# A spectral filter mixed with a 32-head expert lookup: smaller first loads, one transform table, one more row buffer, another order at the end

## The chip, the cores and the metric

One core of one Trainium2 chip runs the kernel. The metric is the device time of one execution in microseconds, the median over several runs. Inputs and output lie in the chip's memory; nothing is computed on the host besides the rearrangement of the inputs and the tables of cosines and sines.

## What is computed

`x` is 2048 x 576. One branch is a two-dimensional spectral filter: forward transform, a product with complex weights, transform back. The other branch is a lookup of experts: for each of 32 heads a query is scored against two lists of 64 keys, the best key of each list gives one row of 4096 (`u` and `v`, 576 numbers each), and gelu(x . u row) times the v row is added up over the heads. A gate per position mixes the two.

```python
g = sigmoid((x * gate_w).sum(-1, keepdims=True))
a = irfft2(rfft2(x) * (w_r + 1j * w_i))
q = einsum("nd,dhc->nhc", x, w_q)                 # 32 heads, 2 halves of 128
i1, i2 = argmax(q1 @ k1.T), argmax(q2 @ k2.T)     # 64 keys each
e = i1 * 64 + i2
b = sum_h gelu(x . u[e]) * v[e]
return g * a + (1 - g) * b
```

## The kernel before

**Tiles.** The 2048 positions are 16 tiles of 128. The first ten (`E_T`) are early tiles, the last six (`L_SEQ`) late tiles, worked on in three pairs (10,11), (12,13), (14,15). The heads are eight chunks of four.

**Score stage.** `load_x` brings 512 positions of one 128-row slice of x transposed; ScalarE writes a rounded high part and VectorE the rest (L356-362). `load_wq` and `build_m` multiply one slice of `w_q` with the keys (L352, L381-397): eight matmuls, a ScalarE copy `mh` (L396), a VectorE remainder `ml` (L397). There are five slices of the 576 inputs; the fifth has only 64 rows, and before the change those are stored twice, so that the fifth slice is loaded as 128 rows. `scores` (L402-455) multiplies, takes the maximum, and turns it into row numbers `ei`.

**Groups.** `group(t, c, ...)` (L480-540) handles one tile and one chunk of four heads. GpSimd gathers four times 128 rows of u and v (590 KB each, L487) into a ring of row buffers: `NG` = 12 plus `NG2` = 1 of the late pools, 13 late. VectorE forms four dot products (L496), ScalarE the gelu (L500), VectorE the factor `a` (L501). Then either VectorE adds the four v rows to the accumulator of the tile (L514), or, where `is_d` holds (even late tiles), ScalarE builds four diagonal matrices (L524) and TensorE adds up 16 matmuls per group in a PSUM tile `sums[t]`. For such a late tile ScalarE copies the PSUM tile to SBUF after the last chunk (L538).

**Spectral stage.** `fold` (L645) brings 16 tiles into the large buffer `BT`; ten `unit`s (L784) run the transforms along the positions with `f2`, `f4`, `f5`, `f6` and `unit_back`, and write `BT` again; `turns` (L677) loads two small tables per unit. `invert(t)` (L808-831) transforms one tile back along d: twelve matmul instructions, a ScalarE copy `pq` (L819), eight more against `krb`, two ScalarE copies scaled with the gate into `ga` (L830, L831). `mix(t)` (L833-836) is one VectorE instruction (L835) and the store. The tables along d, `t_fi`, are twelve planes: six for the way there (`fi[0]`), six with the scale of the way back (`fi[1]`).

**Order.** All work is entered in a planner (`Plan`, L105-233): each job has an engine, a cost, a due time `at` and its dependences. A simulation of the engines takes, on each engine, the ready job with the smallest due time for which buffers of its rings are free, and the order that comes out is written into the program; on the chip each engine and the queues of SP and POOL keep it. Due times of spectral work are spaced by `FPACE`, those of late groups by `TGS`. PSUM is a ring of four tiles of two banks (`p2`), shared by everything. In the time of the late work `xl` is a ring of six buffers, which hold the six late tiles of x and, when one is free, the `ga` of a late tile. Inversions come in the order early tiles, late tiles (L848).

Of the kernel before, what the change touches and what calls it, by code (L numbers as in the profile page):

```python
# [32 lines left out]
def _tables():  # L33
# [10 lines left out]
    def rows(fn, ds):  # L44
        return fn(2 * np.pi * np.outer(ds, k) / D)

    z = np.zeros((P, DF))
    ct = z.copy()
# [4 lines left out]
    fwd = np.stack([  # L53
        rows(np.cos, np.arange(0, 128)), rows(np.cos, np.arange(128, 256)), ct,
        -rows(np.sin, np.arange(0, 128)), -rows(np.sin, np.arange(128, 256)), -st,
    ])
    ck = np.full(DF, 2.0)
    ck[0] = ck[-1] = 1.0
    ck /= S * D

    def irows(fn, ks):
        return fn(2 * np.pi * np.outer(ks, k) / D) * ck[ks][:, None]

    ct = z.copy()
    ct[:33] = irows(np.cos, np.arange(256, 289))
    st = z.copy()
    st[64:96] = irows(np.sin, np.arange(256, 288))
    inv = np.stack([
        irows(np.cos, np.arange(0, 128)), irows(np.cos, np.arange(128, 256)), ct,
        irows(np.sin, np.arange(0, 128)), irows(np.sin, np.arange(128, 256)), st,  # L70
# [12 lines left out]
        "t_fi": c(np.concatenate([fwd, inv]).transpose(1, 0, 2)),  # L83
        "t_f4": c(f4),
        "t_f6": c(f6),
# [167 lines left out]
def tile_kernel(ctx, tc, xn, xT, wqT, kT, wri, uv, gw, t_kr, t_fi, t_f4, t_f6, t_io, out):  # L253
# [84 lines left out]
    gate = pp.tile([P, NT], F32, tag="gate", name="gate")  # L338
    gone = pp.tile([P, NT], F32, tag="gone", name="gone")
# [12 lines left out]
    def load_wq(c, i, at, after=()):  # L352
        w = wq_t[c, i] = buf("uv", ROW, view=lambda x: x.rearrange("p a d -> p (a d)")[:, : 8 * P].rearrange("p (g e) -> p g e", g=8))
        ld(load(P * 4096, 4096), at, lambda: nc.sync.dma_start(w.ap, wqT[c, i]), [w], after=after)

    def load_x(b, i, at, at2):  # L356
        st = buf("uv", ROW, view=lambda x: x[:, 0, :512])
        ld(load(P * 2048, 2048), at, lambda: nc.sync.dma_start(st.ap, xT[:, i, b * 512 : b * 512 + 512]), [st])
        hi = xts[i if i < 4 else 8][b]
        lo, r = (xts[4 + i][b], 0) if i < 4 else (hi, 64)  # L360
        ac(act(512), at2, lambda: actv(hi.ap, st.ap, AF.Copy), [hi], [st])
        dv(dve(512), at2, lambda: vt(lo.ap[r:], st.ap[r:], hi.ap[r:].bitcast(F32), ALU.subtract), [lo], [st, hi])
# [18 lines left out]
    def build_m(c, i, at, after=()):  # L381
        mh, ml = m_t[c, i] = [buf(n, [P, CW], F32R) for n in ("mh", "ml")]
        pm = psum()
        wq = wq_t[c, i]
        pv = lambda: pm.ap.rearrange("p a (g e) -> p (a g) e", e=128)

        def go():
            for g in range(8):
                half = g % 2
                mm(  # L390
                    pv()[:, g, :], wq.ap[:, g, :],
                    kTb.ap[:, half * 64 : half * 64 + 128], start=True, stop=True)
# [3 lines left out]
        ac(act(512), at, lambda: actv(v3(mh), pv()[:, :, :E], AF.Copy), [mh], [pm])  # L396
        dv(dve(512, True), at, lambda: vt(v3(ml), pv()[:, :, :E], v3(mh).bitcast(F32), ALU.subtract), [ml], [pm, mh])  # L397
# [4 lines left out]
    def scores(c, tp, at):  # L402
# [4 lines left out]
        def part(j, i):  # L407
            t = 2 * tp + j
            b = t // 4
            tsl = slice((t % 4) * P, (t % 4) * P + P)  # L410
            mh, ml = m_t[c, i]
            x = xts[i if i < 4 else 8][b]
            seq = [(x, mh), (x, ml)] + ([(xts[4 + i][b], mh)] if i < 4 else [])

            def go():
                for n, (xx, m) in enumerate(seq):
                    mm(ps.ap[:, j, :], xx.ap[:, tsl], m.ap, start=i == n == 0, stop=i == 4 and n == len(seq) - 1)

            use = {id(q): q for pair in seq for q in pair}
            return plan("PE", 0.23 * len(seq), at, go, [(ps, j)], list(use.values()))  # L420
# [59 lines left out]
    def group(t, c, at, ahead, gate_by=()):  # L480
        rows = []
        for k in range(HPC):
# [9 lines left out]
            rows.append(g)  # L492
        z, b, a = (buf(n, [P, HPC]) for n in ("z", "b", "a"))
        x = xs[t]
        for k in range(HPC):
# [3 lines left out]
        zk = [(z, k) for k in range(HPC)]  # L499
        ac(0.18, at - 9, lambda: actv(b.ap, z.ap, AF.Gelu_apprx_tanh), [b], zk, table="gelu")  # L500
        dv(0.08, at, lambda: stt(a.ap, b.ap, 1.0, sw[:, t, c * HPC : c * HPC + HPC], op0=ALU.mult, op1=ALU.mult),  # L501
           [a], [b, ("sw", t, c)])
        new = t not in accs
        if not is_d(t, c):
# [3 lines left out]
            for k in range(HPC):  # L508
# [8 lines left out]
        last = c == NCH - 1  # L517
        if part or t not in sums:
            sums[t] = psum()
        pd = sums[t]  # L520
# [11 lines left out]
        if part or last:  # L532
# [81 lines left out]
    for tag, pool, n in (  # L614
            ("t2", "ip", NT2), ("bt", "ip", 1), ("fi1", "ip", 1), ("krb", "ip", 1),
            ("uv2", "x2", NG2), ("xl", "x2", NT - NE), ("gr", "x2", 1),
            ("f5", "fp", 2), ("kr", "fp", 1), ("fi0", "fp", 1), ("t4", "fp", 2), ("t6", "fp", 2), ("w", "fp", 2)):
# [14 lines left out]
    fi = [buf("fi0", [P, 6, DF]), buf("fi1", [P, 6, DF])]  # L632
# [5 lines left out]
    ld(load(P * 6936, 4096), T0 + 8, lambda: nc.sync.dma_start(fi[0].ap, t_fi[:, 0:6, :]), [fi[0]])  # L638
    ld(0.5, T0 + 15, lambda: nc.sync.dma_start(gw2.ap, gw.partition_broadcast(P)), [gw2])
    ld(load(P * 6936, 4096), T0 + 90, lambda: nc.sync.dma_start(fi[1].ap, t_fi[:, 6:12, :]), [fi[1]])  # L640
# [4 lines left out]
    def fold(t, at):  # L645
        x = xs[t]
        f = buf("f5", [P, ND * P])
        ac(0.17, at, lambda: actv(f.ap[:, 0:385:384], x.ap[:, 0:1].to_broadcast([P, 2]), AF.Copy), [(f, 0)], [x])  # L648
# [15 lines left out]
    def f2(q, at):  # L664
        p = psum()

        def go():
            for r in range(2):
                for n, i in enumerate(((0, 1, 2), (3, 4, 2))[r]):
                    mm(p.ap[:, r, :DF], BT.ap[:, i, :, q], fi[0].ap[:, 3 * r + n, :], start=n == 0, stop=n == 2)  # L670

        plan("PE", 6 * pe(DF), at, go, [p], [fi[0], (BT, "q", q)] + [(BT, "in", t, i) for t in range(NT) for i in range(2)])
# [4 lines left out]
    def turns(k, at):  # L677
        t4 = buf("t4", [P, 3, P])
        t6 = buf("t6", [P, 5, P])
        ld(load(P * 1024, 1024), at - 8, lambda: nc.sync.dma_start(t4.ap[:, 0:2, :], t_f4[k]), [(t4, 0)])  # L680
        ld(load(P * 1024, 1024), at - 8, lambda: nc.sync.dma_start(t6.ap[:, 0:2, :], t_f6[k]), [(t6, 0)])
        ac(act(128), at - 2, lambda: actv(t4.ap[:, 2, :], t4.ap[:, 1, :], AF.Copy, scale=-1.0), [(t4, 1)], [(t4, 0)])
        ac(act(256), at - 2, lambda: actv(t6.ap[:, 2:5:2, :], t6.ap[:, 0:1, :].to_broadcast([P, 2, P]), AF.Copy), [(t6, 1)], [(t6, 0)])
        ac(act(128), at - 2, lambda: actv(t6.ap[:, 3, :], t6.ap[:, 1, :], AF.Copy, scale=-1.0), [(t6, 2)], [(t6, 0)])
        tabs[k] = t4, t6

    def f4(k2, X, at):
# [4 lines left out]
        t4, t6 = tabs[min(k2, 16 - k2)]  # L692
        a, b = (1, 2) if k2 <= 8 else (2, 1)
        p = psum()

        def go():
            T, x, o = t4.ap, X.ap, p.ap
            mm(o[:, 0, :DF], T[:, 0, :], x[:, 0, :], start=True, stop=False)
            mm(o[:, 0, :DF], T[:, a, :], x[:, 1, :], start=False, stop=True)
            mm(o[:, 1, :DF], T[:, 0, :], x[:, 1, :], start=True, stop=False)  # L700
            mm(o[:, 1, :DF], T[:, b, :], x[:, 0, :], start=False, stop=True)

        plan("PE", 4 * pe(DF), at, go, [p], [X, (t4, 0), (t4, 1)])
        return p, w, t6

    def f5(p, w, t6, at):
# [4 lines left out]
        dv(dve(DF), at, lambda: vt(a.ap[:, 0, :], a.ap[:, 0, :], b.ap[:, 1, :], ALU.subtract), [(a, 0)], [b])  # L711
        dv(dve(DF), at, lambda: vt(a.ap[:, 1, :], a.ap[:, 1, :], b.ap[:, 0, :], ALU.add), [(a, 1)], [b])  # L712
        return a, t6

    def f6(k2, zb, t6, at):
        pt = psum()
        u, v = (0, 3) if k2 <= 8 else (2, 1)

        def go():
            z, T = zb.ap, t6.ap  # L720
# [9 lines left out]
        plan("PE", 4 * pe(256) + 4 * pe(128), at, go, [pt], [(zb, 0), (zb, 1), (t6, 0), (t6, 1), (t6, 2)])  # L730
# [10 lines left out]
    def unit_front(k2, at):  # L741
# [8 lines left out]
        ac(act(DF), at, lambda: actv(sr.ap[:, 0, :], psn.ap[:, 1, :DF], AF.Copy, scale=-1.0), [(sr, 0), sr], [psn])  # L750
        ac(act(DF), at, lambda: actv(sr.ap[:, 1, :], psn.ap[:, 0, :DF], AF.Copy), [(sr, 1), sr], [psn])
# [4 lines left out]
    def unit_back(z, at):  # L756
# [19 lines left out]
        dv(dve(256, True), at, lambda: vt(tslot(qs, 0), tm()[:, 1], mainv(pb)[:, 1], ALU.subtract), [(BT, "q", qs, 0)], src + [s_])  # L776
        dv(dve(256, True), at, lambda: vt(tslot(qs, 1), mainv(pb)[:, 0], tm()[:, 0], ALU.subtract), [(BT, "q", qs, 1)], src + [s_])
# [3 lines left out]
        dv(dve(128, True), at, lambda: vt(BT.ap[0:33, 2, :, qs], ta.ap[64:97, 512:], pb.ap[64:97, 1, :P], ALU.subtract), [s_], src)  # L781
        dv(dve(128, True), at, lambda: vt(BT.ap[64:96, 2, :, qs], pb.ap[0:32, 1, :P], ta.ap[0:32, 512:], ALU.subtract), [s_], src)
# [147 lines left out]
```

## Time and profile before

| | |
|---|---|
| median of 3 runs | 1009.44 us (1008.35 to 1010.46) |
| the profiled execution's own time | 1001.24 us |
| its span | 999.5 us |
| mean granted TensorE clock | 0.965 |
| VectorE busy | 916.7 us, 92% of the span |
| TensorE busy | 904.4 us, 90% |
| GpSimd busy (issuing gathers) | 574.4 us, 57% |
| ScalarE busy | 514.6 us, 51% |
| moved by DMA | 348.39 MB, 302.02 MB of them gathered rows |

The profile comes from one execution. In tables of stretches, the columns are the stretch, its length, then for each engine its busy microseconds with the number of instructions begun (PE is TensorE, PEld its weight loads, DVE VectorE, ACT ScalarE, POOL GpSimd), the granted TensorE clock, the busy share of the DMA engines and the GB/s that they moved. In a timeline, a row is start, duration, engine, line and operation, and in brackets the idle time of the engine before it and what ended it. A list of waits gives who waited for whom, the total in us, how often, and the longest. A busy TensorE is not one at its peak, since ends of matmuls are modelled. Each fp32 matmul of the program stands as two instructions.

### The profile page before, as it was taken

The page shows a single profiled execution, that of the slowest core. Times are in us where ns is not written, and L with a number is a line of the kernel's source. Part 1 is how long each engine was busy: PE and PEld are TensorE (multiplying, and loading weights), DVE is VectorE, ACT ScalarE, POOL GpSimd, SP SyncE. Part 2 cuts the span into 40 slices and gives each one's busy share as a digit, 9 for nine tenths or more (in the row PEclk, how much of TensorE's full clock was granted, in tenths as well). Part 3 has the DMA queues.
Part 4 walks back from the last instruction along what each step waited for, and adds up shares of the span by engine and source line. Part 5 has one row for each costly group of instructions (what it writes and reads, how often), then busy time and mean ns, then how long its engine had stood idle before and what let it go on. Part 6 is the DMA issues. An engine that isn't in the chain of part 4 may idle for free. (4 is left out here: it accounts for less than half of the span.)

```text
span 999.5 us, 14406 instructions
## 1 busy us (share of the span) xinstructions
PE 904.4 (90%) x4208; PEld 735.8 (74%) x4208; DVE 916.7 (92%) x2255; ACT 514.6 (51%) x1877; POOL 574.4 (57%) x516
## 2 busy tenths in 40 slices
PE   8997999999999999999998990777999998899993
PEld 7885888878877888887877880665777776677762
DVE  3996999999999999999999999999999999977776
ACT  3874676676666576676666664522212222233331
POOL 0354656565656565755657566476655565676662
PEclk9997999999999999999999996889999999899998
DMA  9987999998989999998999799889999999999994
GB/s 336 336 286 301 349 361 367 358 352 305 392 309 361 371 344 332 395 345 328 386 360 330 291 394 378 340 312 389 394 357 351 357 353 321 349 390 414 398 359 192
DMA packets 93246, 348.39 MB, mean 349 GB/s; under 512 B 10480, under 2 KB 13296, under 8 KB 93168
## 3 DMA queue, kind: packets, MB, share of 16 engines
q0 software_dynamic: 73728, 302.02, 80.9%
q1 hardware_dynamic: 19440, 45.45, 12.3%
q8 instruction: 34, 0.56, 0.2%
q14 instruction: 44, 0.36, 0.1%
HBM read 342.71 MB, written 4.72 MB: 348 GB/s over the span
## 5 line engine op out<-in xcount | busy, mean ns | idle before, releaser
L487 POOL DMA_INDIRECT uv<-uv,ei x512 | 574.2, 1121 | 406.2 <-PE p L313 133.3
L313 PE MATMUL p<-mh,xt 128*128 128x512 f32 x1152 | 383.3, 402 | 9.1 <-ACT sg L435 7.3
L435 ACT ACTIVATE sg<-p,mx 128x64 bf16<-128x64 f32 x1024 | 225.8, 352 | 78.1 <-DVE mx L427 55.7
L514 DVE SCALAR_TENSOR_TENSOR xn<-uv,a,xn 128x576 f32<-128x576 f32 x322 | 262.0, 814 | 1.5
L313 PEld LDWEIGHTS p<-mh,xt 128*128 128x128 f32 x1152 | 218.4, 190 | 59.5 <-ACT sg L435 7.7
L313 PE MATMUL p<-ml,xt 128*128 128x512 f32 x640 | 253.2, 396 | 0.0
L496 DVE SCALAR_TENSOR_TENSOR uv<-uv,xn 128x576 f32<-128x576 f32 x320 | 236.3, 749 | 8.7 <-DMA uv<-uv,ei 6.8
L313 PE MATMUL p<-uv,dg 128*128 128x288 f32 x720 | 194.0, 425 | 29.3 <-ACT dg L524 22.5
L313 PEld LDWEIGHTS p<-uv,dg 128*128 128x128 f32 x720 | 140.8, 199 | 77.9 <-ACT dg L524 29.3
L496 DVE SCALAR_TENSOR_TENSOR uv<-uv,xl 128x576 f32<-128x576 f32 x192 | 141.5, 751 | 0.2
L313 PEld LDWEIGHTS p<-ml,xt 128*128 128x128 f32 x640 | 121.6, 190 | 26.6
L500 ACT ACTIVATE b<-z 128x4 f32<-128x4 f32 x128 | 26.4, 206 | 204.9 <-DVE uv L496 171.4
L313 PE MATMUL p<-fi,bt 128*128 128x289 f32 x384 | 97.7, 408 | 4.4 <-DVE t L710 3.0
L313 PEld LDWEIGHTS p<-fi,bt 128*128 128x128 f32 x384 | 83.5, 242 | 16.5 <-issue 3.7
L313 PEld LDWEIGHTS p<-kT,uv 128*128 128x128 f32 x640 | 77.8, 195 | 7.9 <-issue 4.8
L313 PE MATMUL p<-kT,uv 128*128 128x128 f32 x640 | 78.5, 279 | 5.0 <-DMA uv<-wqT 5.0
L427 DVE TENSOR_REDUCE mx<-p 128x16 f32<-128x1024 f32 x64 | 77.5, 1211 | 3.2 <-PE p L313 3.0
L313 PE MATMUL p<-t,t 128*128 128x289 f32 (+2 forms) x384 | 73.8, 362 | 5.9 <-issue 3.4
L446 ACT ACTIVATE sg<-sg 128x256 bf16<-128x256 bf16 x192 | 72.3, 427 | 1.2
L313 PEld LDWEIGHTS p<-t,t 128*128 128x128 f32 (+1 forms) x384 | 54.1, 165 | 23.9 <-issue 10.7
L524 ACT ACTIVATE dg<-ident,a 128x128 f32<-128x128 f32 x180 | 57.6, 393 | 17.7 <-DVE a L501 14.8
L313 PE MATMUL p<-kr,f 128*128 128x128 f32 x160 | 23.0, 301 | 31.5 <-ACT f L648 26.8
(86 smaller groups left out, 612.1 us busy)
## 6 DMA issues: line engine op xcount, KB each, us to landing
uv<-wqT SPq DMA_DIRECT2D x40, 512.0 KB
uv<-uv,ei POOLq DMA_INDIRECT x512
uv<-xT SPq DMA_DIRECT2D x20, 256.0 KB
w<-wri SPq DMA_DIRECT2D x16, 289.0 KB
out<-xn SPq DMA_DIRECT2D x16, 288.0 KB
xn<-xn SPq DMA_DIRECT2D x10, 288.0 KB
t<-t_f SPq DMA_DIRECT2D x18, 128.0 KB
fi<-t_fi SPq DMA_DIRECT2D x2, 867.0 KB
```

Source lines behind the costliest of these rows:

```text
L313: after("PE", nc.tensor.matmul(*args, **kw))
L427: dv(dve(1024, True), at, lambda: nc.vector.tensor_reduce(mv.ap[:, 2 * tp : 2 * tp + 2, :], ps.ap.rearrange("p a (g e) -> p a g e", e=E), ...
L435: on("ACT", actv(sg.ap[:, j, g, :], ps.ap[:, j, g * E : g * E + E], AF.Sign, bias=mv.ap[:, 2 * tp + j, g : g + 1], scale=-1.0))
L446: ac(act(256), at, lambda b=b: actv(s2()[:, :, b * Q : b * Q + Q], s2()[:, :, b * Q : b * Q + Q], AF.Copy, bias=b / 4), [sg], [])
L487: on("POOL", nc.gpsimd.indirect_dma_start(out=g.ap.rearrange("p a d -> p (a d)"), out_offset=None, in_=uv, in_offset=bass.IndirectOffsetOn ...
L496: dv(0.68, at, lambda k=k, g=rows[k]: stt(g.ap[:, 0, :], g.ap[:, 0, :], 1.0, x.ap, op0=ALU.mult, op1=ALU.mult, accum_out=z.ap[:, k : k + 1 ...
L500: ac(0.18, at - 9, lambda: actv(b.ap, z.ap, AF.Gelu_apprx_tanh), [b], zk, table="gelu")
L514: dv(0.73, at, lambda v=v, s=s: stt(y.ap, v(), s(), y.ap, op0=ALU.mult, op1=ALU.add), [y], [(rows[k], 1), a])
L524: ac(0.3, at - 9, lambda k=k, dg=dg: actv(dg.ap, ident, AF.Copy, scale=a.ap[:, k : k + 1]), [dg], [a, "ident"])
```

## The change

**First loads.** `w_q` and x transposed keep only the 64 rows of the fifth slice: that slice's loads are half as large. The key product of the fifth slice fills 64 partitions; ScalarE copies it twice, to both halves of `mh` (one ScalarE copy more per chunk), and `ml` and its score matmuls use 64 rows. Position blocks 2 and 3 come in one load each slice, and block 3 is split into its parts with block 2's due time (24) instead of its own (`when(3)`, 45.1).

**One table.** The six planes `fi` serve both ways; signs and factors of two move into additions, `fold`, `krb`'s use and a new scale `gsc` of the gate. One 867 KB load goes. The two tables of `turns` come in one load, `tw`.

**Buffers and pace.** The SBUF that becomes free holds one more late row buffer (`NG2` = 2, so 14). `FPACE` goes from 1.7 to 1.4.

**The end.** `INV` inverts late tiles first, then early ones. An even late tile is no longer copied out of PSUM: `mix` reads its `sums` there. The last group, tile 15 and chunk 7, is split in two pairs of heads (`LAST`) and comes after the mix of its tile: its rows are scaled with `gone`, 1 minus the gate, and added to the mixed tile. The store is a job of its own, `send`.

```diff
-        ac(act(512), at, lambda: actv(v3(mh), pv()[:, :, :E], AF.Copy), [mh], [pm])
+        for r in range(0, P, h):
+            ac(act(512), at, lambda r=r: actv(v3(mh)[r : r + h], pv()[:h, :, :E], AF.Copy), [(mh, r)], [pm])
...
     for i in range(ND):
-        load_x(2, i, 15, 24)
+        load_x(2, i, 15, 24, 2)
...
-    for i in range(ND):
-        load_x(3, i, 34, when(3))
...
-        if part or last:
+        if last and not part:
+            accs[t] = pd
+        elif part or last:
...
     def mix(t, at):
         ga, y = gas[t], accs[t]
+        if t in sums:
+            accs[t] = ga
+            half = lambda x: x.rearrange("p (r d) -> p r d", r=2)
+            dv(0.77, at, lambda: stt(half(ga.ap), y.ap[:, :, :288], gone[:, t : t + 1], half(ga.ap), op0=ALU.mult, op1=ALU.add),
+               [(ga, 0), (ga, 1), ga], [y, "gone"])
+            return
...
-    for n, t in enumerate(E_T + L_SEQ):
+    for n, t in enumerate(INV):
...
+        elif t % 2 == 0:
+            group(t, c, at, AHEAD, held)
+            mix(t, at + 9)
+            send(t, at + 9)
+        else:
+            mix(t, at - 4)
+            for ks in LAST:
+                group(t, c, at + 1.65 * ks[0], AHEAD, held, ks, True)
+            send(t, at + 9)
...
-NG2 = 1
+NG2 = 2
...
-FPACE = 1.7
+FPACE = 1.4
...
+INV = L_SEQ + E_T
+LAST = (0, 1), (2, 3)
```

More of the change, by code (lines that the diff above doesn't have):

```diff
@@ L52, in _tables @@
     st[64:96] = rows(np.sin, np.arange(256, 288))
[L53 to L70, printed above, removed]
+    fi = np.stack([
+        c0, rows(np.cos, np.arange(128, 256)), ct,
+        rows(np.sin, np.arange(0, 128)), rows(np.sin, np.arange(128, 256)), st,
     ])
@@ L478, in tile_kernel, with group @@
     sums = {}
-    def group(t, c, at, ahead, gate_by=()):
-        rows = []
-        for k in range(HPC):
+    def group(t, c, at, ahead, gate_by=(), ks=range(HPC), mixed=False):
+        rows = {}
+        for k in ks:
             g = buf(("uv", "uv2"), ROW)
@@ L516, in group @@
         part = t in E_T
[L517 to L520, printed above, removed]
+        last = not any(is_d(t, n) for n in range(c + 1, NCH))
+        if part:
+            pd = psum()
+        elif t in sums:
+            pd = sums[t]
+        else:
+            pd = sums[t] = psum()
         first = part or c == 0
```

172 lines of the change are left out of this document (94 added, 78 removed).

## Prediction

> **What bounds the kernel now.** I read the page's busy times first, then the run in stretches. Columns: stretch, length, busy microseconds of PE, PEld, DVE, ACT and POOL, the granted clock, DMA share, GB/s.
>
> ```profile
> 0.00:30.00 30.00, 25.04 (x142) 22.21 (x143) 11.82 (x18) 13.95 (x34) 0.20 (x4) 1.00 0.96 345
> 30.00:100.00 70.00, 62.48 (x299) 51.36 (x297) 60.20 (x156) 46.73 (x174) 33.52 (x32) 0.93 0.84 302
> 100.00:600.00 500.00, 490.21 (x2324) 401.90 (x2323) 489.13 (x1229) 333.80 (x1295) 305.56 (x269) 0.99 0.94 351
> 600.00:644.00 44.00, 15.70 (x101) 14.12 (x101) 43.73 (x114) 22.59 (x86) 25.75 (x21) 0.69 1.02 390
> 644.00:862.00 218.00, 191.08 (x870) 154.58 (x868) 210.62 (x507) 55.07 (x180) 130.73 (x120) 0.96 0.95 349
> 862.00:975.00 113.00, 109.93 (x448) 84.58 (x448) 84.97 (x200) 39.12 (x104) 73.88 (x68) 1.00 1.00 383
> 975.00:999.50 24.50, 9.98 (x32) 7.00 (x32) 16.26 (x37) 3.37 (x12) 4.71 (x4) 0.84 0.48 187
> ```
>
> VectorE is the bound from 100 to 862: idle 11 us of 500 in the score stage, 7 of 218 in the transforms. In the inversions, 862 to 975, it is idle 28 us and TensorE is full. Two more views of that stage: stretches of the DMA, then who waited.
>
> ```profile
> 865.00:880.00 15.00, 15.00 (x63) 11.65 (x63) 12.41 (x32) 6.20 (x18) 10.57 (x9) 1.00 0.92 310
> 880.00:945.00 65.00, 65.00 (x268) 50.33 (x267) 46.50 (x108) 20.86 (x54) 41.37 (x40) 1.00 1.02 411
> 945.00:955.00 10.00, 10.00 (x43) 7.80 (x42) 7.98 (x21) 3.96 (x11) 5.89 (x6) 1.00 0.95 329
> ...
> 965.00:975.00 10.00, 7.61 (x31) 5.30 (x29) 8.12 (x21) 2.18 (x7) 7.87 (x8) 1.00 0.97 344
> ```
> ```profile
> POOL uv L487 <- PE p L313: 19.3, 8, 3.4
> ...
> DVE xn L835 <- ACT t L831: 7.7, 7, 2.0
> ```
> ```profile
> L496 DVE SCALAR_TENSOR_TENSOR uv<-uv,xl 128x576 f32<-128x576 f32 x192 | 141.5, 751 | 0.2
> 862.68 107.72 PE p L313 x440
> ```
>
> The dot products never wait for gathered rows (0.2 us idle before 192 of them), so VectorE idles there for inversions, through instructions queued behind waiting ones. But the DMA holds 411 GB/s from 880 to 945, far over the 349 of the transform stage: 411 is what it gives, and in the dips beside that stretch GpSimd waits for TensorE to free row buffers (19.3 us in the stage). TensorE and the DMA end this stage nearly together. The end itself, by engine:
>
> ```profile
> 986.19 0.76 DVE L496 SCALAR_TENSOR_TENSOR uv<-uv,xl 128x576 f32<-128x576 f32 x1
> 986.87 0.08 DVE L496 DVE_READ_ACCUMULATOR uv<-uv,xl 128x1 f32 x1
> 991.19 0.82 DVE L835 SCALAR_TENSOR_TENSOR xn<-xn,gone,xl 128x576 f32<-128x576 f32 x1 [4.24 <-ACT xn L538]
> 991.93 0.16 DVE L501 SCALAR_TENSOR_TENSOR a<-b,sw 128x4 f32<-128x4 f32 x1
> 992.12 3.38 DVE L514 SCALAR_TENSOR_TENSOR xn<-uv,a,xn 128x576 f32<-128x576 f32 x4
> 995.54 0.82 DVE L835 SCALAR_TENSOR_TENSOR xn<-xn,gone,xl 128x576 f32<-128x576 f32 x1
> ```
> ```profile
> 984.64 5.84 PE L313 MATMUL p<-uv,dg 128*128 128x288 f32 x16 [5.38 <-ACT dg L524]
> ```
> ```profile
> 990.51 0.65 ACT L538 ACTIVATE xn<-p 128x576 f32<-128x576 f32 x1 [5.05 <-PE p L313]
> 991.06 0.20 ACT L500 ACTIVATE b<-z 128x4 f32<-128x4 f32 x1
> ```
>
> ```profile
> L836 SPq DMA_DIRECT2D out<-xn x16: 332/332/348, 876.5 to 996.4; - x16
> ```
>
> The last dot product ends at 986.95. Its gelu stands on ScalarE behind the copy of tile 14, which waits for TensorE; then come the factor, four additions, the mix and a store of some 3 us (996.4 to 999.5).
>
> **The change part by part.** Sums are against the profiled execution, 1001.24 us (span 999.5, the rest around it). It lies 8.2 us below the median, 1009.44; I carry the difference over unchanged.
>
> *First loads.*
>
> ```profile
> L362 DVE TENSOR_TENSOR xt<-uv,xt 128x512 fp32r<-128x512 f32 (+1 forms) x20 | 13.6, 687 | 13.2 <-ACT xt L361 13.1
> L396 ACT ACTIVATE mh<-p 128x512 fp32r<-128x512 f32 x40 | 24.5, 613 | 19.4 <-remote 9.2 <-PE p L313 7.7 <-issue 2.5
> uv<-wqT SPq DMA_DIRECT2D x40, 512.0 KB
> uv<-xT SPq DMA_DIRECT2D x20, 256.0 KB
> fi<-t_fi SPq DMA_DIRECT2D x2, 867.0 KB
> ```
>
> Ahead of the first score stand 256 + 128 KB less: 0.39 MB / 345 GB/s = 1.1 us. Against it, splitting block 3 early puts five VectorE instructions of 0.69 us = 3.4 us ahead of gathered work. Later VectorE carries any head start to the end. Taken: -0.5; ends -1.1 and +3.4. SP now issues block 3 ahead of the early tiles' x, but as five issues fewer and with five row buffers fewer; no more than the 3.4 already counted.
>
> In the score stage 7 x 256 KB less are loaded, and ScalarE copies 8 times more, 8 x 0.61 = 4.9 us. Both lie beside VectorE's 489 of 500 us; ScalarE is idle 166. Taken: 0. Without that cover, the copies cost 7 chunk starts x 0.61 = +4.3, because score matmuls of slice five and the signs queued on ScalarE wait behind the second copy; the bytes would give 1.8 MB / 351 GB/s = -5.2.
>
> *One table.* One 867 KB load less (near 628, where VectorE is full at 43.7 of 44 us) and nine issues fewer on SP: 0. The loads of `tw` wait for one ring instead of two, as long as `f6` of two units before; they are due a unit ahead, so 0. The extra `gsc` instruction is like L501, 0.16 us: 0.
>
> *Pace.* Due times move nothing by themselves: in the transforms VectorE is full, so what one kind of work gains the other loses. Let the inversions begin X us sooner. Then VectorE owes X us of group work after that point. A group is four L496, on average two L514 (0.82) and an L501: 3.0 + 1.6 + 0.2 = 4.8 us. Half the groups also take 16 diagonal matmul instructions, by the row of all that stand after 862:
>
> ```profile
> L313 PE MATMUL p<-uv,dg 128*128 128x288 f32 x160 | 42.3, 419 | 7.1 <-ACT dg L524 7.1
> ```
>
> That is 42.3 / 10 = 4.2 us a group, so TensorE gets back 4.2 / 9.6 = 0.44 us per us and ends 0.56 X earlier. The DMA gets 2.36 MB per group: 2.36 / 411 GB/s = 5.7 us per 4.8, so its end moves later by 0.2 X. With the last gathers landing just before 986.19, pace alone buys nothing. Taken: 0.
>
> *One more row buffer; TensorE freed sooner.* What can be had is the dips: (411 - 310) x 15 + (411 - 329) x 10 + (411 - 344) x 10 = 3.0 MB, 7.3 us at 411. GpSimd waited there for rows that TensorE held; one buffer in 14 is a fourth of what a diagonal group holds. Taken: half, -3.7; ends 0 and -7.3.
>
> *The end.* After the last dot product there now stand gelu and factor (0.6 with the hand-overs), two additions of 0.82, and the store, some 3.5 with its issue: 986.95 + 0.6 + 1.7 + 3.5 = 992.7, thus -6.8. What is late next is tile 14: its matmuls end at 990.5, the mix from PSUM takes 0.8 to 0.9, the store 3.5: 994.9, -4.6. The added pair costs one factor and one gelu more, and the mix of tile 15 moves ahead: some 1 us of VectorE, if it is not waiting there. If the planner puts the mix of 14 ahead of the last two additions, VectorE waits in order and ends near 990.5 + 0.9 + 1.7 + 3.5 = 996.6, -2.9. Taken: -4.5; ends -6.8 and -0.8 (only the last mix gone).
>
> Sum: -0.5 - 3.7 - 4.5 = -8.7; the profiled execution would take 992.5, the median 1000.7.
>
> **The rivals.**
>
> *A late tile keeps its PSUM tile (slower).* `sums[10]` is now freed by `mix(10)`, which needs an inversion, instead of by L538 at 769:
>
> ```profile
> 769.42 0.65 ACT L538 ACTIVATE xn<-p 128x576 f32<-128x576 f32 x1 [3.36 <-PE p L313]
> ...
> 775.28 0.41 ACT L750 ACTIVATE t<-p 128x289 f32<-128x289 f32 x1 [2.46 <-PE p L313]
> ...
> 796.66 0.41 ACT L750 ACTIVATE t<-p 128x289 f32<-128x289 f32 x1
> ...
> 819.95 0.41 ACT L750 ACTIVATE t<-p 128x289 f32<-128x289 f32 x1 [2.09 <-PE p L313]
> ```
>
> From then on pair two holds another, and the transforms have two tiles of the four instead of three. A unit takes (819.95 - 775.28) / 2 = 22.3 us. If it scales with the tiles it takes 33.5, and four units follow 769: up to 45 us. Inversions are 320 instructions at 107.72 / 440 = 0.245 us, 78.4 us. With a delay d and the 42.3 us of diagonal matmuls, TensorE ends at 862.7 + d + 78.4 + 42.3 - 0.44 d, and two ScalarE copies, mix and store add 5: 988.4 + 0.56 d. It decides (span over 999.5) from d = 20, 5 us per unit; at 45 the span is 1014, the median 1024. For it: TensorE and ScalarE wait for each other in the transforms already. Against it: VectorE, at 210.6 of 218 us, sets their speed, so a unit has time to spare.
>
> *The early stall goes too.*
>
> ```profile
> DVE a L501 <- ACT b L500: 8.0, 2, 4.8
> PEld p L313 <- ACT sg L435: 7.7, 1, 7.7
> PE p L313 <- ACT sg L435: 7.3, 1, 7.3
> ```
>
> Between 74 and 100 VectorE loses 8.0 us in a knot of TensorE, ScalarE and the order of the queues. Another order may not tie it: 8.0 more off, 992.7. It may as well tie another, +8.0, 1008.7, within no change; which, nothing in the profile tells.
>
> *The DMA bounds everything.* If 349 to 351 GB/s were its limit, time would follow bytes: 8 x 256 + 4 x 128 + 867 KB = 3.5 MB, 3.5 / 350 = -10.0 us, and with the end -4.5: 994.9. The 411 GB/s from 880 to 945 and dot products that wait 0.2 us speak against it. The Trainium skill, "DMA: Bandwidth & Descriptors", section "Specifications", gives a limit of about 358 GB/s of memory for one core, by which this rival would hold; the row at 411 is over it, so the measurement decides.
>
> *The change doesn't do what it says.* The buffers may not be used and the mix of 14 sit in the path: then -0.5 - 0.8, 1008.1, no change.
>
> **How the numbers follow.** Forecast 1000.7, chance 0.52, its own range 995 to 1005. The early stall gone, 992.7: 0.14. All by DMA, 994.9: 0.06. Not as said, or another knot of 8 us, 1008 to 1009: 0.10. PSUM held, up to 1024: 0.18. A measurement of this kernel tells 0.2%, 2 us, from no change: faster 0.72, same 0.10, slower 0.18. The best ends together (-1.1 - 7.3 - 6.8 - 8.0) give 986; upward, 1014 takes in the PSUM case to d = 28 and the +4.3 and +3.4; beyond lie some 2 in 10.
>
> **What would show it.** Right: the last gather issued some 4 us sooner, no wait of VectorE for L538, two additions after the last dot product, 411 GB/s without dips. Wrong: first inversion after 862 and ScalarE waits for TensorE grown between 770 and 862 (PSUM); VectorE idle over 11 us between 100 and 600 (the score stage's order); TensorE ending last.

## The result, and the profile after

The changed kernel takes 1049.73 us (median of 4 runs, 1044.09 to 1055.02); the kernel before took 1008.89 us in the runs beside them (1006.11 to 1010.46). The ratio is 1.0407, 95% interval 1.0337 to 1.0477: slower, where I had forecast 1000.7 us.

The profiled execution of the changed kernel took 1053.51 us, its span is 1051.7. The same stretches as before:

```profile
0.00:30.00 30.00, 24.17 (x123) 20.49 (x124) 8.96 (x14) 10.72 (x23) 0.20 (x4) 1.00 0.96 332
30.00:100.00 70.00, 68.91 (x308) 51.69 (x308) 63.69 (x161) 49.79 (x181) 34.78 (x30) 0.98 0.80 283
100.00:600.00 500.00, 496.19 (x2181) 369.07 (x2180) 454.81 (x1133) 311.06 (x1201) 291.76 (x251) 0.99 0.89 325
600.00:644.00 44.00, 41.88 (x161) 29.14 (x159) 42.73 (x113) 30.06 (x114) 26.12 (x24) 1.00 0.82 308
644.00:862.00 218.00, 167.65 (x764) 135.87 (x764) 203.20 (x500) 64.68 (x221) 131.88 (x116) 0.89 0.93 352
862.00:975.00 113.00, 99.58 (x385) 75.67 (x386) 91.49 (x220) 27.38 (x83) 64.81 (x60) 0.88 0.91 342
975.00:1051.70 76.70, 71.02 (x292) 54.95 (x290) 53.60 (x123) 24.18 (x63) 36.15 (x33) 1.00 0.81 308
```

L299 is the helper by which the changed kernel enters every matmul, L313 in the kernel before; the operands tell the matmuls apart. From 600 on, the rows hold an earlier part of the work than the rows of before do, since everything comes some 41 us later.

From 100 to 600 VectorE is idle 45 us instead of 11, and TensorE is busy 496 of 500, but with fewer instructions begun: 2181 against 2324. TensorE is full and does less. The last score matmul tells how much is lost there; first the kernel before, then the changed one:

```profile
601.44 0.40 PE L313 MATMUL p<-ml,xt 128*128 128x512 f32 x1
```
```profile
642.52 0.49 PE L299 MATMUL p<-ml,xt 64*128 64x512 f32 x1
```

It comes 41.1 us later, of 52.2 us that the span has grown. The rest of the run, from there to the end, went from 398.1 to 409.2 us, 11.1 more. By the medians the growth is 40.8 us only: the profiled execution of the kernel before lies 7.7 us under its median, that of the changed kernel 3.8 over, so that the 11.1 us can be scatter in good part. The score stage is the place. The weight loads of TensorE by tile and shape (busy, mean ns, then idle time ahead and what ended it), before and after:

```profile
L313 PEld LDWEIGHTS p<-mh,xt 128*128 128x128 f32 x1152 | 218.4, 190 | 59.5 <-ACT sg L435 7.7 <-issue 2.9
L313 PEld LDWEIGHTS p<-ml,xt 128*128 128x128 f32 x640 | 121.6, 190 | 26.6
```
```profile
L299 PEld LDWEIGHTS p<-mh,xt 128*128 128x128 f32 x1152 | 217.2, 189 | 70.5 <-issue 22.4 <-ACT sg L430 1.4 <-ACT dg L524 0.5
L299 PEld LDWEIGHTS p<-ml,xt 128*128 128x128 f32 x512 | 96.9, 189 | 18.0
L299 PEld LDWEIGHTS p<-ml,xt 64*128 64x128 f32 x128 | 23.4, 183 | 44.5 <-issue 44.2 <-DVE a L498 0.4
```

The 128 loads of 64 rows have 44.2 us of "issue" ahead of them: they wait for nothing that the profile shows. One of them in the timeline: TensorE's matmuls around the fifth slice (two with `mh`, one with `ml`, then what comes next) before, the same after, and the weight loads after:

```profile
203.76 0.63 PE L313 MATMUL p<-mh,xt 128*128 128x512 f32 x2
204.23 0.39 PE L313 MATMUL p<-ml,xt 128*128 128x512 f32 x1
204.46 0.40 PE L313 MATMUL p<-mh,xt 128*128 128x512 f32 x1
```
```profile
203.85 0.62 PE L299 MATMUL p<-mh,xt 128*128 128x512 f32 x2
204.40 0.50 PE L299 MATMUL p<-ml,xt 64*128 64x512 f32 x1
204.82 0.99 PE L299 MATMUL p<-uv,dg 128*128 128x288 f32 x3
```
```profile
203.62 0.42 PEld L299 LDWEIGHTS p<-mh,xt 128*128 128x128 f32 x2
204.39 0.18 PEld L299 LDWEIGHTS p<-ml,xt 64*128 64x128 f32 x1 [0.36 <-issue]
204.82 0.78 PEld L299 LDWEIGHTS p<-uv,dg 128*128 128x128 f32 x4 [0.24 <-ACT dg L524]
```

Before, three matmuls take 0.70 us from start to start (203.76 to 204.46). After, they take 0.97 (203.85 to 204.82), 0.27 us more. The 64-row weight load starts with its own matmul, at 204.39, while the loads ahead of it start 0.23 us before theirs; and the next weight load waits again (0.24 us, here put down to a ScalarE job). 128 such places times 0.27 us are 35 us.

The end of the changed kernel, VectorE first, then TensorE:

```profile
1041.15 0.82 DVE L839 SCALAR_TENSOR_TENSOR xn<-xn,gone,t 128x576 f32<-128x576 f32 x1 [1.77 <-ACT t L829]
1041.88 0.22 DVE L498 SCALAR_TENSOR_TENSOR a<-b,gone,sw 128x2 f32<-128x2 f32 x1
...
1044.28 0.81 DVE L836 SCALAR_TENSOR_TENSOR xl<-p,gone,xl 128x576 f32<-128x576 f32 x1
1045.01 0.75 DVE L492 SCALAR_TENSOR_TENSOR uv<-uv,xl 128x576 f32<-128x576 f32 x1
...
1046.29 1.67 DVE L511 SCALAR_TENSOR_TENSOR xn<-uv,a,xn 128x576 f32<-128x576 f32 x2
1047.88 0.81 DVE L839 SCALAR_TENSOR_TENSOR xn<-xn,gone,t 128x576 f32<-128x576 f32 x1
```
```profile
1040.03 4.04 PE L299 MATMUL p<-uv,dg 128*128 128x288 f32 x16
1043.90 2.11 PE L299 MATMUL p<-t,krb 128*128 128x289 f32 x8
```

There are two additions after the last dot product, as forecast. But TensorE still inverts an early tile at 1043.90, the mixes of early tiles (L839) and of tile 14 (L836) stand on VectorE between the last dot products, and VectorE's last instruction is the mix of an early tile. From the issue of the last gather (1029.25) to the end it takes 22.5 us, 19.8 before (979.74 to 999.5).

### The profile page after: what moved, and what is told of

It is laid out like the page before. It is cut to its first block, busy times and chain, and to the rows that moved or that the text cites. A ratio compares the mean times of both kernels' runs of the same rounds, so it can differ in the third digit from the quotient of the medians.

```text
span 1051.7 us, 14360 instructions
## 1 busy us (share of the span) xinstructions
PE 969.4 (92%) x4208; PEld 736.9 (70%) x4208; DVE 918.5 (87%) x2257; ACT 517.9 (49%) x1883; POOL 585.7 (56%) x516
## 4 chain that ended last, share of the span: by engine, by line
PE 59%; DVE 26%; issue 5%; DMA 5%; ACT 2%; POOL 1%; another core or an unknown queue 1%; SPq 0%; DVEq 0%; POOLq 0%
PE p L299 59%; DVE uv L492 9%; DVE xn L511 8%; DMA uv<-uv,ei 4%; POOL uv L482 1%; DVE mx L422 1%; DVE t L706 1%; DVE t L707 1%; DVE sg L443 1%; DVE bt L772 1%; DMA uv<-wqT 1%; ACT sg L430 1%; DVE t L708 0%; DVE p L369 0%
## 5 line engine op out<-in xcount | busy, mean ns | idle before, releaser
L482 POOL DMA_INDIRECT uv<-uv,ei x512 | 585.5, 1144 | 444.8 <-PE p L299 145.1
L299 PE MATMUL p<-mh,xt 128*128 128x512 f32 x1152 | 391.2, 409 | 1.1 <-ACT sg L430 1.1
L299 PEld LDWEIGHTS p<-mh,xt 128*128 128x128 f32 x1152 | 217.2, 189 | 70.5 <-issue 22.4
L299 PE MATMUL p<-ml,xt 128*128 128x512 f32 (+1 forms) x640 | 265.5, 415 | 0.0
L492 DVE SCALAR_TENSOR_TENSOR uv<-uv,xn 128x576 f32<-128x576 f32 x320 | 237.3, 753 | 19.8 <-DMA uv<-uv,ei 17.8
L299 PE MATMUL p<-uv,dg 128*128 128x288 f32 x720 | 197.1, 430 | 15.0 <-ACT dg L524 9.3
L299 PEld LDWEIGHTS p<-uv,dg 128*128 128x128 f32 x720 | 144.1, 202 | 61.2 <-ACT dg L524 12.4
L299 PEld LDWEIGHTS p<-ml,xt 128*128 128x128 f32 (+1 forms) x640 | 120.3, 188 | 62.5 <-issue 44.2
L299 PE MATMUL p<-fi,bt 128*128 128x289 f32 x384 | 102.4, 422 | 11.5 <-ACT t L748 7.1
L299 PEld LDWEIGHTS p<-fi,bt 128*128 128x128 f32 x384 | 85.6, 247 | 26.3 <-ACT t L748 7.5
L299 PE MATMUL p<-kT,uv 128*128 128x128 f32 (+1 forms) x640 | 83.6, 287 | 5.8 <-DMA uv<-wqT 5.8
L299 PEld LDWEIGHTS p<-kT,uv 128*128 128x128 f32 (+1 forms) x640 | 76.7, 187 | 13.7 <-issue 10.2
L390 ACT ACTIVATE mh<-p 128x512 fp32r<-128x512 f32 (+1 forms) x48 | 28.8, 600 | 53.1 <-PE p L299 44.4
L299 PE MATMUL p<-kr,f 128*128 128x128 f32 x160 | 24.0, 307 | 27.8 <-ACT f L647 24.4
L299 PE MATMUL p<-tw,t 128*128 128x256 f32 (+1 forms) x256 | 42.3, 345 | 5.5 <-DVE t L708 2.8
```

The source lines that it names most:

```text
L299: after("PE", nc.tensor.matmul(*args, **kw))
L390: ac(act(512), at, lambda r=r: actv(v3(mh)[r : r + h], pv()[:h, :, :E], AF.Copy), [(mh, r)], [pm])
L482: on("POOL", nc.gpsimd.indirect_dma_start(out=g.ap.rearrange("p a d -> p (a d)"), out_offset=None, in_=uv, in_offset=bass.IndirectOffsetOn ...
L492: dv(0.68, at, lambda k=k, g=rows[k]: stt(g.ap[:, 0, :], g.ap[:, 0, :], 1.0, x.ap, op0=ALU.mult, op1=ALU.mult, accum_out=z.ap[:, k : k + 1 ...
```

## The experiments

The kernel before took 990 to 1005 us in the later groups of runs, each on one chip, so every number below is a ratio to the kernel before on the same chip, with its interval.

### 128 rows for `ml` in the changed kernel: e1_ml128

```diff
+        if i == 4:
+            ac(act(512), at, lambda: actv(v3(ml)[h:], pv()[:h, :, :E], AF.Copy, scale=0.0), [(ml, 1)], [pm])
...
-            seq = [(x, mh, P), (x, ml, h)] + ([(xts[4 + i][b], mh, P)] if i < 4 else [])
+            seq = [(x, mh, P), (x, ml, P)] + ([(xts[4 + i][b], mh, P)] if i < 4 else [])
```

> The changed kernel, but the low part of the fifth slice's key matrix (ml) fills all 128 rows again: rows 64 to 127 are set to zero by one more copy on ScalarE per chunk (8 in all), and the 128 score matmuls that had 64 rows have 128. Loads, ScalarE's second mh copy, the late tiles and the end stay as changed. Theory 1 (each 64-row score matmul between 128-row ones costs TensorE about 0.28 us, 128 of them 36 us, and that makes TensorE the bound of the score stage): the last score matmul ends near 602 to 610 instead of 643, the time falls from 1049.7 to between 1005 and 1018. Theory 2 (the loss is made by the late tiles, which keep their PSUM buffers): the last score matmul may move, the time stays over 1035. Theory 4 (the doubled mh copies on ScalarE stall the score stage): no gain, the time is 1050 to 1055, since ScalarE has eight copies more.

Measured: 1.0187 (1.0152 to 1.0222). The loss falls from 4.1% to 1.9%, on eight ScalarE copies more. TensorE has air again from 100 to 600:

```profile
100.00:600.00 500.00, 477.64 (x2235) 388.83 (x2233) 472.26 (x1183) 327.56 (x1256) 311.48 (x260) 0.98 0.91 335
```

Theory 1 holds for about half of the loss. The last score matmul came at 614.6 us, not at 602 to 610, and the time stayed above its range: something else in the score stage costs too.

### 64 rows for `ml` in the kernel before: e2_before_ml64

```diff
-                    mm(ps.ap[:, j, :], xx.ap[:, tsl], m.ap, start=i == n == 0, stop=i == 4 and n == len(seq) - 1)
+                    mm(ps.ap[:, j, :], xx.ap[:k, tsl], m.ap[:k], start=i == n == 0, stop=i == 4 and n == len(seq) - 1)
```

Here `k` is 64 for the fifth slice's `ml` and 128 otherwise.

> The kernel before, with one edit: the fifth slice's ml score matmul reads 64 rows of both operands instead of 128 (it leaves out the product of the two low parts, as the changed kernel does). The order of all engines, all loads and all copies are those of before. Theory 1: the last score matmul ends 30 to 40 us later than 601.8 and the time is 1035 to 1047. Theories 2, 3 (other orders) and 4: no change, 1006 to 1011.

Measured: 1.0348 (1.0316 to 1.0379), 33 us by the medians, from this one edit. It cuts the work of 128 matmuls in half and changes no order. The last score matmul starts at 630.17 us; with 96 rows, on the same chip and in the same order (`e4_before_ml96` below), it starts at 593.26. Its weight loads read as in the changed kernel:

```profile
L313 PEld LDWEIGHTS p<-ml,xt 64*128 64x128 f32 x128 | 23.4, 183 | 44.5 <-issue 42.7 <-DVE xn L514 1.4 <-DVE uv L496 0.4
```

### Half as many changes of the row count: e3_before_pairs

```diff
+            turn = j == 1 and tp not in (0, 7)
+            i = (4, 0, 1, 2, 3)[i] if turn else i
...
+            if j == 1 and i == 4:
+                seq = seq[::-1]
```

> The kernel before with the 64-row matmuls as in the run of that edit alone, but put two by two: in each pair of token tiles the first tile ends with its 64-row matmul and the second begins with its own, so that there are about half as many changes between 128 and 64 rows (60 of the 64 pairs stand together) with as many 64-row matmuls. If the price is paid at the change of the row count (drain): about half of the loss, 1020 to 1028. If it is paid by each 64-row matmul (slower by itself): the same as without pairing, 1035 to 1047. Theories 2 to 4: 1006 to 1011.

Measured: 1.0144 (1.0115 to 1.0173), 14.6 us instead of 33. The price is paid at the change, not by the matmul. A pair in its timeline:

```profile
332.71 0.61 PE L313 MATMUL p<-mh,xt 128*128 128x512 f32 x2
333.25 0.73 PE L313 MATMUL p<-ml,xt 64*128 64x512 f32 x2
333.91 0.73 PE L313 MATMUL p<-mh,xt 128*128 128x512 f32 x2
```

Four matmuls take 1.20 us from start to start; at the 0.233 us of 128-row ones they would take 0.93. That is 0.27 us again, now for two.

### 96 rows: e4_before_ml96

The edit is that of the 64 rows, with `k` 96.

> The kernel before with the fifth slice's ml score matmul on 96 rows (it leaves out half of the product of the two low parts). If what costs is the other row mode of the array (64 rows as a tile of its own), 96 rows need the full height and cost nothing: 1006 to 1011. If any row count under 128 costs, 1035 to 1047.

Measured: 0.9982 (0.9956 to 1.0008). 96 rows cost nothing that shows:

```profile
L313 PEld LDWEIGHTS p<-ml,xt 96*128 96x128 f32 x128 | 24.2, 189 | 5.5
```

So it is not that fewer than 128 rows are used. It is 64 rows between matmuls of more.

### Which part holds the rest: e5_late_only, e6_x_part, e7_w_part

`e5_late_only` has the whole score stage of before and all late parts of the change; the next two add one half of the new first loads to it. In `e6_x_part` x is loaded as changed:

```diff
+        src = lambda: xT[:, i, b * 512 : (b + n) * 512] if i < 4 else x5[:, b * 512 : (b + n) * 512]
```

In `e7_w_part` the weights are loaded and built as changed, with `ml` filled to 128 rows:

```diff
+        ld(load(P * e * 32, e * 32), at, lambda: nc.sync.dma_start(w.ap, wqT[c, i] if i < 4 else wq5[c]), [w], after=after)
```

> The changed kernel with its whole score stage as before (loads of x and of the query weights, builds and score matmuls of the fifth slice); kept are the one table, the faster pace, the second late row buffer, the late even tiles held in PSUM, the late tiles inverted first and the split end. With 128-row matmuls the changed kernel was still 1.0187 times the time before, and its last score matmul came 21 us late. If what is left of the loss is made in the score stage by the fifth slice's loads, builds and the order that they bring (theory 4), this run stands at 0.990 to 1.006 of before, with the last score matmul at 590 to 604. If it is made by the late parts (theory 2, the held PSUM buffers, or 3, pace and order), it stays at 1.013 to 1.025.

> The run with the score stage as before, plus only the new loads of x (fifth slice on 64 rows, the third and fourth token blocks in one load). Theory 4 in the form that the builds make the loss (two mh copies one after the other on ScalarE, in the way of the softmax): no change to the run without it. If the merged early load of the fourth token block makes it (buffers and DMA time taken early): 1.010 to 1.025 with the lateness there by 150 us.

> The run with the score stage as before, plus only the new loads and builds of the query weights' fifth slice, with the low part filled up to 128 rows by a copy of zeros (so 16 copies on ScalarE more than before, as in the run of the whole change with 128-row matmuls). Theory 4 with the builds: 1.010 to 1.025, most of the loss left, ScalarE's mh copies and the waits for them longer. Otherwise the same as the run without it.

Measured: 1.0022 (0.9986 to 1.0057), 1.0070 (1.0026 to 1.0115) and 1.0245 (1.0187 to 1.0302). The late parts together change nothing that shows, the loads of x at most a little, the loads and builds of the weights cost 2.2% over the first. That is a second loss, next to the 64-row matmuls. The parts don't add up to the digit: `e1_ml128` has the loads of x as well and stands at 1.0187, under `e7_w_part`, but within the noise of the two.

### Copies or order: e9_two_copies, e10_plan_only, e13_order_of_e7, e14_copies_old_order, e15_copies_full_width

The first two take the kernel before. One lets ScalarE make the fifth slice's `mh` in two copies; the other lets the planner count both, but the chip runs one.

```diff
+        for r in range(0, P, h):
+            ac(act(512), at, lambda r=r: actv(v3(mh)[r : r + h], pv()[r : r + h, :, :E], AF.Copy), [(mh, r)], [pm])
```
```diff
+        for r in range(0, P, h):
+            plan("ACT", act(512), at, lambda r=r: r or on("ACT", actv(v3(mh), pv()[:, :, :E], AF.Copy)), [(mh, r)], [pm])
```

> The kernel before, in which ScalarE makes the fifth slice's mh in two copies of 64 rows instead of one of 128 (eight copies of some 0.6 us more in the run, 4.8 us in all, one ahead of the first build's subtraction in each chunk); loads, weights and matmuls as before. The run with only the new loads and builds of the weights stood at 1.0245 of before. Theory 4 in the strict form (the second copy itself, at the chunk's start, holds up VectorE and TensorE): 1.010 to 1.025. Theory 5 (it is the order that the planner writes once the job list differs, or the loads, and not the copies): 0.997 to 1.008.

> The kernel before in the order that the planner writes for the two copies, but with the second copy left empty: the planner counts it, the chip never runs it, and the first copy fills all 128 rows as before. All engines run the same instructions as before, in the other order of the two-copy run. If the two-copy run is slow and the copies cause it: this one is at 0.997 to 1.004. If the order causes it: the same as the two-copy run within 0.004.

Measured: 1.0030 (1.0001 to 1.0059) and 1.0037 (1.0013 to 1.0061). One copy more per chunk is not it: the second run has no instruction more than before and loses as much as the first, within 0.4%, so that what they lose comes with the order.

The other three go back to `e7_w_part` and cross order and instructions, on the base of `e5_late_only`. `e13_order_of_e7` has its jobs with the instructions of before:

```diff
+            plan("ACT", act(512), at, lambda r=r: r or on("ACT", actv(v3(mh), pv()[:, :, :E], AF.Copy)), [(mh, r)], [pm])
+        if i == 4:
+            plan("ACT", act(512), at, lambda: None, [(ml, 1)], [pm])
```

`e14_copies_old_order` has one job as before with the new instructions in it; `e15_copies_full_width` is the same with the loads and builds of before:

```diff
+        def split():
+            for r in range(0, P, h):
+                on("ACT", actv(v3(mh)[r : r + h], pv()[:h, :, :E], AF.Copy))
+
+        def rest():
+            on("DVE", vt(v3(ml)[:h], pv()[:h, :, :E], v3(mh)[:h].bitcast(F32), ALU.subtract))
+            if i == 4:
+                on("ACT", actv(v3(ml)[h:], pv()[:h, :, :E], AF.Copy, scale=0.0))
```

> Every engine runs its instructions in the order of the run with only the new loads and builds of the weights (1.0245 of before), but the fifth slice is loaded, built and copied as before: full loads, 128-column builds, one mh copy, no copy of zeros. Theory 5 (the order costs it): 1.015 to 1.030. Theory 6 (the new instructions cost it: the copies, the 64-column matmuls, the half loads): 0.997 to 1.008, as the run with the score stage of before (1.0022).

> The opposite: the order of the run with the score stage as before (1.0022), but the fifth slice's half loads, 64-column builds, two mh copies and copy of zeros, each put where the one of before stood. Theory 5 (order): 0.998 to 1.008. Theory 6 (instructions): 1.015 to 1.030. If both runs come out near 1.010, both have a part.

> As the run with the old order and the new instructions, but with full loads and 128-column builds: only the three ScalarE copies in a row are new. Theory 6 with the copies: the same as that run. Theory 6 with the 64-column matmuls or the half loads: 0.998 to 1.006 while that run is at 1.015 or over. Theory 5: 0.998 to 1.006, and that run too.

Measured: 1.0111 (1.0058 to 1.0164), 1.0098 (1.0056 to 1.0139) and 1.0079 (1.0034 to 1.0124). Neither theory holds alone. Over the 1.0022 of the base, the order costs 0.9% (give or take 0.6%) and the new instructions in the old order 0.8% (give or take 0.5%). The second number can't be carried over as it stands. In `e14_copies_old_order` and `e15_copies_full_width` the copy of zeros (`ml`) is entered behind VectorE's subtraction, and ScalarE stands there, 11.6 and 11.9 us in all. In `e7_w_part` it hardly does; first `e14_copies_old_order`, then `e7_w_part`:

```profile
L393 ACT ACTIVATE ml<-p 64x512 fp32r<-64x512 f32 x8 | 4.7, 589 | 11.6 <-DVE ml L391 11.6
```
```profile
L388 ACT ACTIVATE ml<-p 64x512 fp32r<-64x512 f32 x8 | 4.7, 591 | 1.4 <-DVE ml L389 1.3
```

So it is not shown whether the copies cost by themselves or by this wait. That the 64-column builds and half loads cost little (1.0098 against 1.0079) is likely only. In the new order the new instructions cost 1.3% (1.0245 against 1.0111, give or take 0.8%); by which of them stays open. The changed kernel itself has no copy of zeros, since it does not fill `ml`.

### The late parts by themselves: e8_psum_copy, e11_table_buffer, e12_end_only

`e8_psum_copy` is `e5_late_only` with this edit, and the old mix:

```diff
-        if last and not part:
-            accs[t] = pd
-        elif part or last:
+        if part or last:
```

`e11_table_buffer` is the kernel before with the one table, `tw`, and

```diff
-NG2 = 1
+NG2 = 2
-FPACE = 1.7
+FPACE = 1.4
```

`e12_end_only` is the kernel before with the held PSUM tiles, the new mix and

```diff
+INV = L_SEQ + E_T
+LAST = (0, 1), (2, 3)
```

> The run with the score stage as before, but the three late even tiles are copied out of PSUM by ScalarE when their sums are done, and mixed from there, as before the change. Theory 2 (held PSUM buffers slow the transforms): 5 to 15 us faster than the run without it. Otherwise the same within 3 us, or a little slower through the three copies.

> The kernel before with only the one table along d, the merged twiddle tables, the faster pace and the second late row buffer; score stage and end as before. The prediction gave the buffer -3.7 us (0 to -7.3) and table and pace nothing: 0.993 to 1.000. A theory that the gathers after the score stage are bound by the DMA whatever buffers there are: 0.998 to 1.002.

> The kernel before with only the new end: late tiles inverted first, late even tiles held in PSUM and mixed from there, the last group in two pairs on a mixed tile. The prediction gave it -4.5 us (-6.8 to -0.8): 0.993 to 0.999. The rival that tile 14's mix stands ahead of the last dot product on VectorE and waits for TensorE, as the trace of the changed kernel shows: 1.000 to 1.006.

Measured: 1.0021 (0.9991 to 1.0050), 1.0039 (1.0012 to 1.0066) and 1.0076 (1.0045 to 1.0107). In the change as a whole the held PSUM tiles cost nothing that shows (1.0022 with them, 1.0021 without), although the first `krb` matmul of an inversion comes 289.8 us after the last score matmul with them and 275.0 without. Table and buffer alone bring no gain, and the new end alone loses; both lie above all the ranges named for them.

### What takes the end its gain: e17_end_psum_copy, e18_end_both, e19_mix14_last

Each adds one edit to the run before it, starting from `e12_end_only`: the copy out of PSUM, the order of the inversions, and tile 14's copy after the last gelu with its mix after the last addition.

```diff
-        if last and not part:
-            accs[t] = pd
-        elif part or last:
+        if part or last:
```
```diff
-INV = L_SEQ + E_T
+INV = E_T + (15, 14, 10, 11, 12, 13)
```
```diff
+            tail["copy"]()
+            mix(14, at + 9, [tail["add"]])
+            send(14, at + 9)
```

> The kernel before with only the new end (1.0076 of before), but the late even tiles are copied out of PSUM by ScalarE as before; late tiles are still inverted first, the last group still in two pairs on a mixed tile. If the held PSUM tiles cost the end its gain: 0.995 to 1.002, with the first inversion some 12 us earlier after the last score matmul (274 instead of 286). If the early tiles' mixes between the last dot products cost it: 1.004 to 1.010.

> As the run with the copy out of PSUM, and in addition the inversions go early tiles, then 15, 14, then 10 to 13, so that only tile 14's mix can stand near the last dot products. If the mixes in between cost the end its gain, this run shows the predicted end: 0.993 to 0.999, from the last gather's issue to the end 15 to 18 us instead of 19.8 to 22. If the order of the inversions does not matter: the same as the run without it within 0.003.

> As the run with both edits at the end (1.0010 of before), but tile 14's copy out of PSUM, mix and store come after the gelu and the additions of the last pair of heads. In that run VectorE stood 3.5 us at the mix with the last dot product behind it; the copy started at 986.9, so that copy, mix and store should end some 2.9 us sooner than 994.4. If that wait is what the end is bound by: 0.995 to 1.000, and 15 to 16.5 us from the last gather's issue to the end instead of 18.6. If TensorE's last 16 matmuls just come later: the same as without it.

Measured: 1.0037 (1.0013 to 1.0061), 1.0010 (0.9984 to 1.0035), 0.9971 (0.9947 to 0.9994). The first inversion's `krb` matmul, in `e12_end_only` and in `e17_end_psum_copy`, where the last score matmuls start at 598.94 and 594.68:

```profile
885.06 1.14 PE L313 MATMUL p<-t,krb 128*128 128x289 f32 x4
```
```profile
863.32 1.87 PE L313 MATMUL p<-t,krb 128*128 128x289 f32 x7
```

286.1 us after the last score matmul with the held tiles, 268.6 without: the hold delays the inversions by 17.5 us, and the whole by perhaps 4 (1.0076 against 1.0037, whose intervals overlap).

In `e17_end_psum_copy` the early tiles' mixes are over before the last gather is issued (969.67). What stands in the way at the end is tile 14's mix, with the last two dot products behind it:

```profile
984.12 0.82 DVE L846 SCALAR_TENSOR_TENSOR xn<-xn,gone,xl 128x576 f32<-128x576 f32 x1 [5.25 <-ACT xn L543]
```

With the other order of the inversions (`e18_end_both`) the time from the last gather to the end falls from 22.6 to 18.6 us, and one dot product is left behind that mix:

```profile
987.57 0.82 DVE L846 SCALAR_TENSOR_TENSOR xn<-xn,gone,xl 128x576 f32<-128x576 f32 x1 [3.49 <-ACT xn L543]
988.31 0.75 DVE L497 SCALAR_TENSOR_TENSOR uv<-uv,xl 128x576 f32<-128x576 f32 x1
988.99 0.08 DVE L497 DVE_READ_ACCUMULATOR uv<-uv,xl 128x1 f32 x1
...
989.60 1.67 DVE L516 SCALAR_TENSOR_TENSOR xn<-uv,a,xn 128x576 f32<-128x576 f32 x2
```

Tile 14's mix waits 3.49 us for TensorE, and the last dot product stands behind it, 12.5 us after the last gather was issued (975.81); in the next run it starts 9.1 us after. With the mix moved (`e19_mix14_last`):

```profile
980.16 1.68 DVE L517 SCALAR_TENSOR_TENSOR xn<-uv,a,xn 128x576 f32<-128x576 f32 x2
...
982.74 0.82 DVE L851 SCALAR_TENSOR_TENSOR xn<-xn,gone,xl 128x576 f32<-128x576 f32 x1 [0.91 <-ACT xn L544]
```

From the issue of the last gather to the end it takes 16.9 us (969.77 to 986.7) instead of 18.6, and 19.8 before the change; I had expected 15 to 16.5, but ScalarE still waits for TensorE there. This version is faster than both kernels, by 2.9 us over the kernel before (0.6 to 5.3).

## Why the prediction was wrong

**The step that failed is the score stage, "Taken: 0".** It priced the bytes and the eight ScalarE copies, and said that both lie beside VectorE's 489 of 500 us. It left out the third thing that the change does there, the score matmul on 64 rows, and so priced it at nothing without a reason. The runs show 0.27 us for each visit to 64 rows, 33 us in all in the kernel before (1.0348) and, from 1.0407 against 1.0187, 2.2% or some 22 us in the changed one (on two chips, each against the kernel before on the same chip). That it is less there, because other losses leave TensorE some room, is likely and not shown. The cover was thin and stood in the quoted row: TensorE was busy 490.21 of 500 us, so that anything over 10 us on it had to show. "VectorE is the bound from 100 to 862" stood beside a TensorE that was busy 1 us more; I treated it as free. The sign named for a wrong score stage, VectorE idle over 11 us there, is what came, with 45.

The Trainium skill, "TensorEngine Tiling (Array Packing)", section "Key Properties", says that a change of the tiling mode drains TensorE, and the page's list has 64 rows as another mode than 128. The trace agrees in the wait (0.36 us of "issue" ahead of the 64-row load); no view names it a drain. The 96-row run without a price fits too. The page gives no price; here it is 0.27 us for a visit, there and back.

The Trainium skill, "TensorE: Matmul & The Clock Gate", section "Why this matters for your kernels", says that a single matmul on 32 rows takes as long as one on 128. No run here has 32 rows; on 96 rows it is so (0.9982). That rule alone would have led to 0 again.

**The same step, its upper end of +4.3.** It was made from the copies alone. With 128-row matmuls the loads and builds of the weights cost 2.2% over 1.0022 in `e7_w_part`, and 1.7% in `e1_ml128`, together with the loads of x: 17 to 22 us. Some 0.9% is the order that the planner writes for all engines; the rest comes with the new instructions, and by which of them is open. The prediction had the order as a cause to watch ("the score stage's order") but at 8 us, from one stall.

**First loads, -0.5 (-1.1 to +3.4).** The loads of x alone moved 1.0022 to 1.0070; the intervals overlap, so that a cost of a few us is likely only.

**One table and pace, 0; row buffer, -3.7.** Together alone 1.0039 (+4 us). That is as much as the order alone moved the kernel in `e10_plan_only`, so that the runs don't tell whether the buffer gives something back. The gain of 3.7 us did not come.

**The end, -4.5.** The split gives 2.9 us of the 4.5, but only once three things are changed: the held tiles (-0.4%), the order of the inversions (-0.3%), tile 14's mix ahead of the last dot product (-0.4%). The intervals of neighbours overlap each time, so that each size alone is only likely; from 1.0076 to 0.9971 the three together are shown, and for the third the timeline shows the wait go. The prediction named the third, with 996.6 as its end, but put the waiting mix ahead of the additions only, not of the dot product, and took it as the less likely case.

**The rivals.** The mechanism of the held PSUM tiles came as told: the first `krb` matmul stands 290.9 us after the last score matmul instead of 271.2. The rival's rule, 988.4 + 0.56 d, gives 999.4 for d = 19.7, no change, and 1.0022 is that. The DMA as the bound of everything fell: 3.5 MB less were moved, in more time. The early stall is not set by the order of the instructions: the run with 96 rows has before's order, on another chip, and no such stall. First the kernel before, then that run:

```profile
74.00:100.00 26.00, 18.72 (x74) 14.69 (x72) 17.27 (x49) 11.62 (x49) 12.87 (x13) 0.80 0.81 301
```
```profile
74.00:100.00 26.00, 24.29 (x118) 19.66 (x117) 24.89 (x66) 17.38 (x73) 18.27 (x17) 1.00 1.01 398
```

The granted clock is 0.80 in the one and 1.00 in the other; whether the stall lowers the clock or the clock makes the stall is open.

## What to carry to other kernels

Price every matmul shape that a change makes new on TensorE, whatever the number of its multiplications; a shape on 64 rows between others of 128 costs about 0.27 us per visit here, so fill it up (96 rows cost nothing here) or put such matmuls together. Where two engines are busy 489 and 490 of 500 us, both are the bound, and neither hides anything. In an order written ahead, look at what each waiting instruction has behind it on its engine, and expect some 0.4 to 1% from a new order alone before believing a gain of that size.

## What the runs showed of the hardware

- A matmul on 96 rows costs as much as one on 128 (0.9982). One on 64 rows among those of 128 costs 0.27 us more, and two together cost that once.
- The price shows as "issue" ahead of the 64-row weight load: 42.7 to 44.2 us for 128 of them.
- The kernel before took between 990 and 1009 us (medians) in the seven groups of runs. A time from one group can't be set against a time from another.
